# The guard for tiny weights of w_out and w3 on ScalarE, and the early stage's on-chip transfers begun from ScalarE's queue

## The chip, the cores and the metric

The kernel runs on one core of one Trainium2 chip. The metric is device microseconds of one execution. The engines are called PE (TensorE matmul; PEld is its weight load), DVE (VectorE), ACT (ScalarE), POOL (GpSimd) and SP (SyncE, which here only issues DMAs; its queue is SPq in the profile).

## What is computed

A block-causal attention over 8 batches, 8 heads, 576 positions and 64 columns a head (blocks of 64), and then a gated MLP on its output, all in float32:

```python
scores = scale * np.matmul(q, k.transpose(0, 1, 3, 2))
scores = np.where(mask, scores, -1000000000.0)      # mask: block_i >= block_j
attn = softmax(scores)                              # with 1e-09 added to the sum
x = np.matmul(attn, v)                              # as (4608, 512)
a = x @ w1                                          # w1, w2: (512, 1024)
b = x @ w2
h = a * b @ w3                                      # w3: (1024, 1024)
return h @ w_out                                    # w_out: (1024, 512)
```

q and k are drawn with a spread of about 0.4, v with 0.1. The weights arrive as float64, seen as pairs of 32-bit integers.

## The kernel before

The work goes by pairs of heads, n = 0 to 31, four to a batch; within a pair the heads are j = 0 and 1. A matmul with full precision is made of products of a high part (float32r) and a low part (the rest), as in the three products per weight tile in `gen_moe`.

**Two stages.** In the early stage, pairs 0 to 3 (`EARLY`), the attention of batch 0 runs beside the preparation of all weights (`gen_w`). `w_out` comes in 8 tiles, `w3` in 16 (two for each of eight columns of blocks, m = 0 to 7), `w1` and `w2` in 8 each: 40 tiles of 128 x 512 weights. For each m, eight products on PE (L358) make 128 rows of w3 x w_out, named w0 to w7; ACT and DVE split the sum into `wh` and `wl` (L346, L347). The first, w0, needs all of `w_out` and the two tiles of w3 for m = 0. In the late stage pairs 4 to 31 are mixed with the MLP of the batch before, and PE's order is the one in which the code is written. Its first MLP products (ab, L381) need xh and xl of pairs 0 to 3, the last of which is x of pair 3.

**One weight tile** (`load_w`, L122 to L143): SP issues the load into one of five `wraw` buffers; ACT takes the absolute value of the upper words (L135) into one of six `wbits` buffers; DVE raises it to at least 2^-15 (L136, the guard for tiny weights, which keeps the exponent of the next step from running below its range), shifts and masks it (L137), puts the sign and the top bit of the exponent in (L138) and adds three bits of the lower word (L141). For w1 and w2 the result goes on to ACT and DVE, which split it into high and low (L147, L148); for w_out and w3 it is used as it is.

**One pair of the early stage.** `shift_mask` finds the row maxima by products mx on PE and reductions m on DVE (L179, L183, L185), transposes them (mt, L187) and ACT writes them as `ms` (L189). `prep_qk` casts q and k to `qk` (L157), copies that high part to the other half of the partitions with a transfer inside the chip (qk<-qk, L206) and subtracts the low part on DVE (L207). `shift` writes `ms` as a row of `qk` with a second transfer inside the chip (qk<-ms, L196). Then PE forms s (L230), ACT exp (pe, L238), PE x (L269); DVE transposes the sums (tr, L309) and scales x (L320 to L323), and `finish_x` splits it into xh and xl (L332, L333). All these transfers, like the loads, stand in SP's queue.

**What sets the order.** In the early stage a scheduler orders each engine's instructions from the plans `EARLY_PLAN` and from priorities: steps of the attention go ahead of the weights. Each queue then runs in its order, and an instruction that waits holds up all behind it.

Of the kernel before, what the change touches and what calls it, by code (L numbers as in the profile page):

```python
# [7 lines left out]
F32 = mybir.dt.float32  # L8
# [3 lines left out]
AF = mybir.ActivationFunctionType  # L12
ALU = mybir.AluOpType
# [3 lines left out]
P = 128  # L17
B, H, S, D = 8, 8, 576, 64
BLK = 64
NB = S // BLK  # L20
# [8 lines left out]
EARLY = NPAIR  # L29
SCALE = 0.125  # L30
BIG = 8.0e9

# [24 lines left out]
def block_causal_attention__then__gated_mlp_kernel(ctx, tc, qkv, consts, ident_in, w1, w2, w3t, wout, out_t):  # L59
    nc = tc.nc  # L60
    w1, w2, w3t, wout = (w.bitcast(I32) for w in (w1, w2, w3t, wout))

    cpool = ctx.enter_context(tc.tile_pool(name="cpool", bufs=1))
# [18 lines left out]
    qk = [cpool.tile([P, 4, S], F32R, name=f"qk{j}") for j in range(2)]  # L82
# [28 lines left out]
    def open_late():  # L111
# [7 lines left out]
        tl["gh"] = pool.tile([P, NF, HALF], F32R, name="gh")  # L119
        tl["gl"] = pool.tile([P, NF, HALF], F32R, name="gl")  # L120

    def load_w(dst, src, k):  # L122

        t = tl["early"].tile([P, 1024], F32, tag="wraw", name="wraw", bufs=5)
        u = tl["early"].tile([P, 512], F32, tag="wbits", name="wbits", bufs=6)
        wide = t.bitcast(I32)
        nc.sync.dma_start(out=wide.rearrange("p (k w) -> p k w", k=k), in_=src)  # L130
        wide = wide.rearrange("p (c two) -> p c two", two=2)
        low, high = wide[:, :, 0], wide[:, :, 1]
        bits = u.bitcast(I32)
        V = nc.vector
        nc.scalar.activation(u, high.bitcast(F32), AF.Abs)  # L135
        V.tensor_scalar(out=u, in0=u, scalar1=2.0**-15, scalar2=None, op0=ALU.max)  # L136
        V.tensor_scalar(out=bits, in0=bits, scalar1=3, scalar2=0x3FFFFFF8, op0=ALU.logical_shift_left, op1=ALU.bitwise_and)  # L137
        V.scalar_tensor_tensor(out=bits, in0=high, scalar=-0x40000000, in1=bits, op0=ALU.bitwise_and, op1=ALU.bitwise_or)  # L138
        if dst is None:
            dst = u.unsqueeze(1)  # L140
        V.scalar_tensor_tensor(out=dst.bitcast(I32), in0=low.rearrange("p (k w) -> p k w", k=k), scalar=29,  # L141
                               in1=bits.rearrange("p (k w) -> p k w", k=k), op0=ALU.logical_shift_right, op1=ALU.bitwise_or)
        return u  # L143

    def load_split(dst_h, dst_l, src):
        val = load_w(None, src.unsqueeze(1), 1)
        nc.scalar.copy(dst_h, val)  # L147
        nc.vector.tensor_tensor(out=dst_l, in0=val, in1=dst_h, op=ALU.subtract)  # L148
# [6 lines left out]

    def cast(n, dst, src, act):
        (nc.scalar.copy if 0 < n <= EARLY or act else nc.vector.tensor_copy)(dst, src)  # L157

    ms_of = {}

    def shift_mask(n):
        r = raw_of[n]
        rqk = r[:, 0 : 2 * S].rearrange("p (t s) -> p t s", t=2)
        kb = work.tile([P, S], BF16, tag="kb", name=f"kb{n}")
        cast(n, kb, rqk[:, 1, :], CAST[1])
        for j in range(2):
            cast(n, qd[own[j], :, own[j]], rqk[own[j], 0, :].rearrange("p (i r) -> p i r", r=BLK), CAST[2])
# [21 lines left out]
        nc.scalar.mul(out=ms[0:NB], in_=mt[0:NB, 0:P], mul=-1.0)  # L189
        ms_of[n] = ms  # L190
        shift(n, 0)
        yield

    def shift(n, j):
        row = qk[j][oth[j].start : oth[j].start + 1, 1, :].rearrange("p (i r) -> p i r", r=BLK)
        nc.sync.dma_start(out=row.bitcast(F32), in_=ms_of[n][0:NB, j * BLK : (j + 1) * BLK].bitcast(F32))  # L196

    def prep_qk(n, j):
        rqk = raw_of[n][:, 0 : 2 * S].rearrange("p (t s) -> p t s", t=2)
        o, x = own[j], oth[j]  # L200
        if j == 1:
            shift(n, 1)
        high, low = qk[j][o, 0::3, :], qk[j][o, 1:3, :]
        cast(n, high, rqk[o], CAST[0])
        yield
        nc.sync.dma_start(out=qk[j][x, 0::2, :].bitcast(F32), in_=high.bitcast(F32))  # L206
        (nc.vector if n <= EARLY else nc.gpsimd).tensor_tensor(out=low, in0=rqk[o], in1=high, op=ALU.subtract)  # L207
        yield

# [126 lines left out]
    def gen_w(wp):  # L336
        wo = tl["wo"]
        for k in range(NF):
            load_w(wo[:, k : k + 1, :], wout[k * P : (k + 1) * P, :].unsqueeze(1), 1)
            yield  # L340
# [8 lines left out]
        for m in range(NF):  # L349
            t3 = wp.tile([P, NF, P], F32, tag="w3", name="w3", bufs=2)  # L350
            for k in range(0, NF, 4):
                src = w3t[k * P : (k + 4) * P, 2 * m * P : 2 * (m + 1) * P].rearrange("(k p) f -> p k f", p=P)
                load_w(t3[:, k : k + 4, :], src, 4)
                if k == 0:
                    yield
            acc = ps_m.tile([P, 512], F32, tag="psm", name=f"w{m}")
            for k in range(NF):
                nc.tensor.matmul(acc, t3[:, k, :], wo[:, k, :], start=(k == 0), stop=(k == NF - 1))  # L358
            pending.append((m, acc))
            if len(pending) > 1:  # L360
                evacuate()
            yield
            next(rows1)
            yield
# [48 lines left out]
    open_early(wp)  # L413
    fill(shift_mask(0), 100)
    fill(prep_qk(0, 0), 100)
    for j in range(2):
        prep_v(0, j)
# [3 lines left out]
    def pair(n):  # L421
# [5 lines left out]
        last = n + 1 == NN  # L427
        masks = iter(()) if last else shift_mask(n + 1)
        own_qk = prep_qk(n, 1)
        next_qk = iter(()) if last else prep_qk(n + 1, 0)  # L430
        for j in range(2):
            xps = ps_x.tile([P, 1024], F32, tag="psx", name=f"x{n}_{j}")
# [60 lines left out]
def _layout(q, k, v, moe_w1, moe_w2, moe_w3, moe_w_out):  # L493
# [12 lines left out]
    for c in range(4):  # L506
        consts[1 + c, 0, 2 * c * BLK : (2 * c + 1) * BLK] = 1.0
        consts[1 + c, 1, (2 * c + 1) * BLK : (2 * c + 2) * BLK] = -BIG
    return {
# [27 lines left out]
```

## Time and profile before

| | |
|---|---|
| median of 3 runs | 1007.41 us (1006.82 to 1007.84) |
| the profiled execution | 1008.37 us, its span 1006.6 us |
| PE busy | 961.6 us, 96% of the span |
| PEld busy | 886.1 us, 88% |
| DVE busy | 718.8 us, 71% |
| ACT busy | 547.9 us, 54% |
| POOL busy | 521.1 us, 52% |
| DMA | 80.39 MB, mean 80 GB/s |

The shares are means over both stages. The profile's slices of 25 us show DVE at 70 to 99% and DMA at 50 to 80% in the first five and DVE near 75% and DMA near 20% later. So a stage is read by itself: the busy time of each engine in a stretch, then the engine's rows in order of time, in which a bracket gives the idle time ahead of a row and what ended it. Busy times of neighbours overlap by a little, since the next instruction starts while the last one drains; what one of them adds in a full queue is the distance from start to start.

### The profile page before, as it was taken

The numbers are of one execution on the slowest core, as the hardware profiler recorded it, in microseconds if no ns is written. First come the engines' busy times: TensorE is split into PE (matmuls) and PEld (weight loads), VectorE is DVE, ScalarE is ACT, GpSimd is POOL, SyncE is SP. The second block draws the span as 40 slices with busy tenths as digits, with TensorE's granted clock in tenths as the row PEclk, the third lists the DMA queues.
The fourth block names the chain that finished last, engine by engine and source line by source line (L and its number), as shares of the span: only waits on it lengthen the run. The fifth ranks groups of instructions, "written<-read, shape, count | busy, mean of one in ns | idle before, by whom it ended". The sixth has DMA issues, their size and how long they took to land.

```text
span 1006.6 us, 18165 instructions
## 1 busy us (share of the span) xinstructions
PE 961.6 (96%) x6594; PEld 886.1 (88%) x6624; DVE 718.8 (71%) x1356; ACT 547.9 (54%) x1433; POOL 521.1 (52%) x525
## 2 busy tenths in 40 slices
PE   4699958999999999999999999999999999999998
PEld 2354548999999999999999999999999999999998
DVE  7999997767777777777777767777777777774100
ACT  4655755555565655555555566555555655653211
POOL 0000006667665766666666657576666766573211
PEclk9799978999999999999999999999999999999999
DMA  8776522122212221221222222212212222110000
GB/s 247 240 257 195 170 82 61 55 80 61 85 57 78 61 74 38 70 73 56 78 61 85 61 74 61 84 32 67 73 58 76 61 85 61 37 24 25 1 25 24
DMA packets 36409, 80.39 MB, mean 80 GB/s; under 512 B 4384, under 2 KB 20896, under 8 KB 36320
## 3 DMA queue, kind: packets, MB, share of 16 engines
q1 hardware_dynamic: 36320, 79.23, 26.5%
q8 instruction: 52, 0.85, 0.4%
q14 instruction: 37, 0.30, 0.1%
HBM read 50.76 MB, written 9.44 MB: 60 GB/s over the span
## 4 chain that ended last, share of the span: by engine, by line
PE 60%; DVE 23%; ACT 9%; issue 6%; DMA 2%; DVEq 0%; ACTq 0%
PE ab L381 23%; PE o L397 20%; DVE pl L248 7%; PE s L230 6%; PE x L285 4%; PE mx L179 3%; DVE g L388 2%; ACT ph L246 2%; PE w L358 2%; ACT p L245 2%; DVE m L183 2%; DVE wbits L138 1%; DVE x L323 1%; DVE rb L322 1%; DVE qk L157 1%
## 5 line engine op out<-in xcount | busy, mean ns | idle before, releaser
L251 POOL TENSOR_TENSOR rsum<-rsum,p 128x448 f32<-128x448 f32 x224 | 178.3, 796 | 120.4 <-ACT p L245 113.6
L248 DVE TENSOR_TENSOR pl<-p,ph 128x448 fp32r<-128x448 f32 x168 | 150.9, 911 | 64.1 <-ACT ph L246 63.2
L389 ACT CAST gh<-g 128x288 fp32r<-128x288 f32 x128 | 55.5, 433 | 219.3 <-DVE g L388 219.3
L390 POOL TENSOR_TENSOR gl<-g,gh 128x288 fp32r<-128x288 f32 x128 | 108.3, 846 | 123.0 <-ACT gh L389 122.9
L230 PE MATMUL s<-qk 128*128 128x288 f32 (+4 forms) x768 | 160.7, 317 | 9.2 <-DMA qk<-ms 3.5
L381 PE MATMUL ab<-xh,w1h 128*128 128x288 f32 x512 | 152.0, 297 | 6.8 <-ACT xh L332 6.8
L381 PE MATMUL ab<-xh,w2h 128*128 128x288 f32 x512 | 154.1, 301 | 0.0
L397 PE MATMUL o<-gh,wh 128*128 128x288 f32 x512 | 153.4, 300 | 0.0
L381 PE MATMUL ab<-xh,w1l 128*128 128x288 f32 x512 | 151.6, 296 | 0.0
L381 PE MATMUL ab<-xl,w2h 128*128 128x288 f32 x512 | 151.5, 296 | 0.0
L381 PE MATMUL ab<-xl,w1h 128*128 128x288 f32 x512 | 151.5, 296 | 0.0
L381 PE MATMUL ab<-xh,w2l 128*128 128x288 f32 x512 | 151.4, 296 | 0.0
L397 PE MATMUL o<-gl,wh 128*128 128x288 f32 x512 | 150.8, 295 | 0.0
L397 PE MATMUL o<-gh,wl 128*128 128x288 f32 x512 | 150.8, 295 | 0.0
L207 POOL TENSOR_TENSOR qk<-raw,qk 64x1152 fp32r<-64x1152 f32 x54 | 144.3, 2672 | 2.0
L220 POOL TENSOR_TENSOR vs<-raw,vs 128x320 fp32r<-128x320 f32 x56 | 49.9, 891 | 174.2 <-ACT vs L157 174.2
L230 PEld LDWEIGHTS s<-qk 128*128 128x128 f32 (+1 forms) x768 | 116.9, 184 | 26.1 <-issue 6.1
L183 DVE TENSOR_REDUCE m<-mx 128x1 f32<-128x512 f32 (+6 forms) x320 | 128.6, 449 | 15.8 <-PE mx L179 13.2
L246 ACT ACTIVATE ph<-s 128x288 fp32r<-128x288 f32 x336 | 131.3, 392 | 0.0
L388 DVE TENSOR_TENSOR g<-ab,a 128x288 f32<-128x288 f32 x128 | 57.7, 451 | 74.4 <-PE ab L381 71.2
L245 ACT ACTIVATE p<-s 128x448 f32<-128x448 f32 x224 | 85.5, 382 | 45.8 <-PE s L230 44.2
L285 PE MATMUL x<-ph,vs 128*128 128x128 f32 x336 | 104.1, 319 | 0.0
(71 smaller groups left out, 2141.6 us busy)
## 6 DMA issues: line engine op xcount, KB each, us to landing
raw<-in_qkv SPq DMA_DIRECT2D x32, 896.0 KB
qk<-qk SPq DMA_DIRECT2D x64, 288.0 KB
out_t<-o SPq DMA_DIRECT2D x64, 144.0 KB
wraw<-in_w3t SPq DMA_DIRECT2D x16, 512.0 KB
wraw<-in_w SPq DMA_DIRECT2D x16, 512.0 KB
wraw<-in_wout SPq DMA_DIRECT2D x8, 512.0 KB
qk<-ms SPq DMA_DIRECT2D x64, 2.2 KB
cst<-in_consts SPq DMA_DIRECT2D x1, 288.0 KB
```

The source lines that it names most:

```text
L183: nc.vector.reduce_max(m[:, col : col + 1], sc, axis=AX.X)
L207: (nc.vector if n <= EARLY else nc.gpsimd).tensor_tensor(out=low, in0=rqk[o], in1=high, op=ALU.subtract)
L230: nc.tensor.matmul(t[ks, at : at + q1 - q0], qk[j][:, 2 + s, kr], qk[j][:, s, q0:q1], start=(s == 0), stop=(s == 1))
L245: nc.scalar.activation(p32, t[ks, at : at + w], AF.Exp, scale=SCALE)
L246: nc.scalar.activation(ph[ks, o : o + w], t[ks, at : at + w], AF.Exp, scale=SCALE)
L248: nc.vector.tensor_tensor(out=low, in0=p32, in1=ph[ks, o : o + w], op=ALU.subtract)
L251: nc.gpsimd.tensor_tensor(out=r, in0=r, in1=p32, op=ALU.add)
L285: nc.tensor.matmul(xps[:, to : to + w], v[:, c, :], pr[:, a : a + w], start=(u < 2 and s == 0), stop=(u in (0, len(PV) - 1) and s == len(p ...
L381: nc.tensor.matmul(t[:, 0:HALF], l[:, c, fs], r, start=(c == 0 and s == 0), stop=(c == NC - 1 and s == 2))
L388: nc.vector.tensor_tensor(out=g32, in0=acc[1][:, 0:HALF], in1=a32, op=ALU.mult)
L390: nc.gpsimd.tensor_tensor(out=gl[:, f, :], in0=g32, in1=gh[:, f, :], op=ALU.subtract)
L397: nc.tensor.matmul(t[:, 0:HALF], l[:, f, es], r[:, f, :], start=(f == 0 and s == 0), stop=(f == NF - 1 and s == 2))
```

## The change

For w_out and w3 (where `load_w` is given a destination) the guard becomes one ACT instruction on the upper 16 bits of each word, seen as unsigned integers: relu(top - 0x3800), with the constant in a new tile `floor` of one column. The subtracted bits are among those that the next step masks out. For w1 and w2 the guard stays on DVE. The transfers inside the chip, L206 and L196 before, are issued from ACT's queue for pairs 0 to 4 and from SP's for the rest.

```diff
+U16 = mybir.dt.uint16
...
+    floor = cpool.tile([P, 1], F32, name="floor")
+    nc.vector.memset(floor, -float(0x3800))
...
         nc.scalar.activation(u, high.bitcast(F32), AF.Abs)
-        V.tensor_scalar(out=u, in0=u, scalar1=2.0**-15, scalar2=None, op0=ALU.max)
+        if dst is None:
+            V.tensor_scalar(out=u, in0=u, scalar1=2.0**-15, scalar2=None, op0=ALU.max)
+        else:
+            top = u.bitcast(U16).rearrange("p (c two) -> p c two", two=2)[:, :, 1]
+            nc.scalar.activation(top, top, AF.Relu, bias=floor)
...
+    def queue(n):
+
+        return nc.scalar if n <= EARLY else nc.sync
...
-        nc.sync.dma_start(out=row.bitcast(F32), in_=ms_of[n][0:NB, j * BLK : (j + 1) * BLK].bitcast(F32))
+        queue(n).dma_start(out=row.bitcast(F32), in_=ms_of[n][0:NB, j * BLK : (j + 1) * BLK].bitcast(F32))
...
-        nc.sync.dma_start(out=qk[j][x, 0::2, :].bitcast(F32), in_=high.bitcast(F32))
+        queue(n).dma_start(out=qk[j][x, 0::2, :].bitcast(F32), in_=high.bitcast(F32))
```

The scheduler makes a new order of it on every engine. In the names below, s0_1 is s of pair 0, head 1, and the last number is that of a buffer; lines are those of the kernel in question. First ACT around the mask row ms of pair 1, before:

```order
L238 ACTIVATE pe0_1_280<-s0_1_309 128x320
L238 ACTIVATE pe0_1_280<-s0_1_322 128x192
L238 ACTIVATE pe0_1_280<-s0_1_322 64x64
L157 CAST qk1_85<-raw1_147 64x2x576
L135 ACTIVATE wbits_294<-wraw_293 128x512
L216 COPY ve1_144<-raw1_147 128x5x64
L135 ACTIVATE wbits_315<-wraw_314 128x512
L135 ACTIVATE wbits_330<-wraw_329 128x512
L189 ACTIVATE ms1_272<-mt1_270 9x128
L135 ACTIVATE wbits_392<-wraw_391 128x512
L157 CAST kb2_375<-raw2_353 128x576
L157 CAST qd_88<-raw2_353 64x9x64 x2
```

and after the change:

```order
L251 ACTIVATE pe0_1_282<-s0_1_311 128x320
L140 ACTIVATE wbits_332<-wraw_331 128x512
L202 ACTIVATE ms1_274<-mt1_272 9x128
L145 ACTIVATE wbits_332<-wbits_332,floor_97 128x512
L209 DMA qk0_84<-ms1_274 1x9x64
L251 ACTIVATE pe0_1_282<-s0_1_324 128x192
L251 ACTIVATE pe0_1_282<-s0_1_324 64x64
L166 CAST kb2_377<-raw2_355 128x576
L166 CAST qd_88<-raw2_355 64x9x64
L140 ACTIVATE wbits_394<-wraw_393 128x512
L166 CAST qd_88<-raw2_355 64x9x64
```

The transfer qk0<-ms1 is now ACT's, right behind the guard of the second w3 tile (wbits_332); the cast of qk1 and the copy ve1 have gone behind these rows, and kb and qd of pair 2 stand behind that guard.

PE around the first product of w3 and w_out, w0, before:

```order
L230 MATMUL s1_0_379<-qk0_84 128x288
L269 MATMUL x0_1_279<-pe0_1_280,ve1_144 128x192
L230 MATMUL s1_0_383<-qk0_84 128x288
L269 MATMUL x0_1_279<-pe0_1_280,ve1_144 128x64
L187 MATMUL mt1_270<-ident_79,m1_213 9x128
L358 MATMUL w0_337<-wo_100,w3_313 128x512 x8
L230 MATMUL s1_0_383<-qk0_84 128x288
L230 MATMUL s1_0_379<-qk0_84 128x288
L358 MATMUL w1_422<-wo_100,w3_405 128x512
```

and after:

```order
L282 MATMUL x0_1_281<-pe0_1_282,ve1_146 128x448
L243 MATMUL s1_0_381<-qk0_84 128x288
L282 MATMUL x0_1_281<-pe0_1_282,ve1_146 128x320
L371 MATMUL w0_339<-wo_102,w3_315 128x512 x8
L282 MATMUL x0_1_281<-pe0_1_282,ve1_146 128x192
L243 MATMUL s1_0_385<-qk0_84 128x288
L282 MATMUL x0_1_281<-pe0_1_282,ve1_146 128x64
L243 MATMUL s1_0_381<-qk0_84 128x288
L243 MATMUL s1_0_385<-qk0_84 128x288
L371 MATMUL w1_424<-wo_102,w3_407 128x512 x2
```

Two products of x of pair 0 and one of s of pair 1 have gone behind w0, and its mt ahead of them (not in the rows any more).

DVE around the first two tiles of w3 (w3_313 before, w3_315 after), before:

```order
L141 SCALAR_TENSOR_TENSOR wo_100<-wraw_293,wbits_294 128x512
L138 SCALAR_TENSOR_TENSOR wbits_315<-wraw_314,wbits_315 128x512
L136 TENSOR_SCALAR wbits_330<-wbits_330 128x512
L141 SCALAR_TENSOR_TENSOR w3_313<-wraw_314,wbits_315 128x512
L137 TENSOR_SCALAR wbits_330<-wbits_330 128x512
L309 STREAM_TRANSPOSE tr0_1_355<-x0_1_279 64x576
L138 SCALAR_TENSOR_TENSOR wbits_330<-wraw_329,wbits_330 128x512
L310 TENSOR_SCALAR rr0_150<-tr0_1_355 64x18
L136 TENSOR_SCALAR wbits_392<-wbits_392 128x512
L141 SCALAR_TENSOR_TENSOR w3_313<-wraw_329,wbits_330 128x512
```

and after:

```order
L147 SCALAR_TENSOR_TENSOR wbits_317<-wraw_316,wbits_317 128x512
L146 TENSOR_SCALAR wbits_332<-wbits_332 128x512
L150 SCALAR_TENSOR_TENSOR w3_315<-wraw_316,wbits_317 128x512
L147 SCALAR_TENSOR_TENSOR wbits_332<-wraw_331,wbits_332 128x512
L150 SCALAR_TENSOR_TENSOR w3_315<-wraw_331,wbits_332 128x512
L142 TENSOR_SCALAR wbits_394<-wbits_394 128x512
```

Between the guard's neighbours there is no L136 any more, and the transpose tr of pair 0, head 1, which stood between the two tiles of w3, has gone behind the next tiles. As counted over the whole order, 16 guards are left on DVE (L142 after the change), 24 are on ACT (L145), and ACT has 20 transfers (10 of L209 and 10 of L219).

## Rows read from the trace of the kernel before

**Rows 1.** Stretches: length; busy PE, PEld, DVE, ACT, POOL; clock; DMA share; GB/s
```profile
11.50:41.60 30.10, 17.91 (x69) 11.03 (x67) 28.93 (x64) 17.79 (x35) 0.00 (x0) 0.92 0.81 253
40.00:45.00 5.00, 3.24 (x4) 1.52 (x5) 4.88 (x12) 3.30 (x6) 0.00 (x0) 0.50 0.87 286
41.60:153.00 111.40, 97.40 (x313) 52.76 (x316) 108.18 (x219) 65.15 (x127) 2.15 (x2) 0.91 0.57 176
41.70:138.00 96.30, 93.58 (x300) 49.69 (x303) 93.82 (x192) 59.14 (x116) 0.00 (x0) 0.96 0.64 200
153.50:1006.60 853.10, 844.53 (x6209) 821.55 (x6236) 576.03 (x1069) 459.76 (x1264) 516.75 (x516) 1.00 0.20 59
```
**Rows 2.** Timeline of PE: start, length, instruction, count, idle before and its end
```profile
34.36 0.49 PE L269 MATMUL x<-pe,ve 128*128 128x192 f32 x2
...
34.91 0.43 PE L269 MATMUL x<-pe,ve 64*128 64x64 f32 x2
...
41.76 9.58 PE L358 MATMUL w<-wo,w 128*128 128x512 f32 x16 [4.41 <-DVE w L141]
...
61.65 7.11 PE L358 MATMUL w<-wo,w 128*128 128x512 f32 x16
...
85.19 0.96 PE L230 MATMUL s<-qk 128*128 128x448 f32 x4 [0.48 <-ACT pe L238]
...
102.78 0.59 PE L269 MATMUL x<-pe,ve 128*128 128x192 f32 x2 [0.54 <-ACT pe L238]
...
114.71 0.40 PE L230 MATMUL s<-qk 128*128 128x288 f32 x1 [0.24 <-ACT pe L238]
...
129.86 0.79 PE L230 MATMUL s<-qk 128*128 128x288 f32 x4 [0.70 <-DVE qk L207]
...
143.43 1.09 PE L230 MATMUL s<-qk 128*128 128x288 f32 x3 [3.50 <-DMA qk<-ms]
...
153.50 0.61 PE L381 MATMUL ab<-xh,w1h 128*128 128x288 f32 x1 [6.82 <-ACT xh L332]
```
**Rows 3.** Timeline of DVE
```profile
33.64 1.36 DVE L207 TENSOR_TENSOR qk<-raw,qk 64x1152 fp32r<-64x1152 f32 x1 [0.66 <-ACT qk L157]
...
114.38 0.76 DVE L136 TENSOR_SCALAR wbits<-wbits 128x512 f32<-128x512 f32 x2
...
130.56 0.78 DVE L309 STREAM_TRANSPOSE tr<-x 64x576 f32<-64x576 f32 x1
...
151.24 1.42 DVE L323 TENSOR_TENSOR x<-x,rb 128x576 f32<-128x576 f32 x1
```
**Rows 4.** Groups by line to 153.5 us: count, busy us, mean ns, idle before
```profile
L136 DVE TENSOR_SCALAR wbits<-wbits 128x512 f32<-128x512 f32 x40 | 16.5, 417 | 0.3 <-ACT wbits L135 0.3
...
L135 ACT ACTIVATE wbits<-wraw 128x512 f32<-128x512 f32 x40 | 26.9, 677 | 19.0 <-DMA wraw<-in_w3t 9.4 <-DMA wraw<-in_w 4.9 <-DMA wraw<-in_wout 2.5
```
**Rows 5.** Stretches for one line alone, L136 on DVE, L135 on ACT
```profile
11.50:41.60 30.10, 4.18 (x10) 0.92 0.81 253
...
11.50:41.60 30.10, 6.45 (x10) 0.92 0.81 253
```
**Rows 6.** Issues on SP to 160 us: count, shortest, median, longest ns
```profile
L196 SPq DMA_DIRECT2D qk<-ms x10: 751/794/887, 17.1 to 141.7; - x10
...
L206 SPq DMA_DIRECT2D qk<-qk x10: 602/660/687, 6.5 to 137.2; - x10
```
**Rows 7.** Timeline of ACT
```profile
32.46 1.15 ACT L157 CAST qk<-raw 64x1152 fp32r<-64x1152 f32 x1
...
35.38 0.46 ACT L216 COPY ve<-raw 128x320 f32<-128x320 f32 x1 [1.07 <-PE x L269]
...
37.56 0.65 ACT L135 ACTIVATE wbits<-wraw 128x512 f32<-128x512 f32 x1
...
39.85 0.67 ACT L157 CAST kb<-raw 128x576 bf16<-128x576 f32 x1 [1.63 <-DMA raw<-in_qkv]
40.42 1.35 ACT L157 CAST qd<-raw 64x576 bf16<-64x576 f32 x2
```

## The prediction

> **What bounds the kernel now.** I read the table by stretch first. After 153.5 us PE is busy for 844.5 of 853.1 us, so that part is bound by TensorE; its order is fixed, and the change moves only its start [rows 1]. What can move is the first 153.5 us. There the same table shows two different regimes. From 11.5 to 41.6 us DVE is busy for 28.9 of 30.1 us and PE for 17.9: the weights are being unpacked and PE waits for the first block of w3 with all of w_out. From 41.7 to 138 us both are full, PE 93.6 and DVE 93.8 of 96.3 us. Then DVE alone is full again until x of pair 3 is scaled, while PE idles.
>
> The timeline of PE says the same in rows. It waits 4.41 us for DVE's first w3 tile and begins the products w = w_out x w3 at 41.76; from there to 129.86 its idle pieces are 0.48, 0.54, 0.24 and 0.70 us, 2.0 us in 88 [rows 2]. So in that stretch nothing that makes DVE faster can give more than 2.0 us: PE has no more idle time to lose. After it PE waits 3.5 us and then 6.82 us for xh, which hangs on DVE's product x at 151.24 [rows 2, 3]. This is the second place where DVE decides.
>
> **Part 1: the guard goes from DVE to ACT, 24 of 40 times.** L136 costs 417 ns on average, but two in a row take 0.76 us, so a further one adds 0.34 us: that is its price in a full queue [rows 3, 4]. 24 of them are 8.2 us of DVE. Ten lie ahead of the first w3 tile, 8 for w_out and 2 for w3, 10 x 0.34 = 3.4 us; they are the ten of the stretch to 41.6 [rows 5]. The other 14, 4.8 us, lie beside a full PE and can give at most the 2.0 us above.
>
> On ACT no row has a 16-bit integer operand. The nearest is the Abs on the same 512 columns, L135, 677 ns [rows 4]; below it stands its share in a full queue, 10 in 6.45 us [rows 5]; above it I allow twice 677 ns, since nothing shows that a 16-bit, every-second-element operand is as fast. I take 677, as operation, columns and partitions are those of the row. That makes 24 x 0.68 = 16.3 us more of ACT. The guard also stands between Abs and DVE's shift, one more ACT instruction of latency for each tile; six buffers of wbits cover it as long as ACT runs ahead.
>
> The Trainium skill, "ScalarE: Activation LUTs", Rules for kernel authors, tells one to do relu and max on VectorE, not on ScalarE. The durations above agree with it, and by it alone the move would cost 24 x (0.677 - 0.417) = 6.2 us of engine time and end at 1013.6 us.
>
> **Part 2: 20 transfers begin on ACT.** On SP one issue of qk<-qk takes 660 ns and one of qk<-ms 794 ns [rows 6]. The after kernel has ten of each on ACT, 14.5 us; no row shows an issue on ACT, so the bounds are nothing (it passes while the instruction ahead still runs) and those durations plus the cast's own length where the issue waits for the cast just ahead; I take SP's durations. SP is freed of the same 14.5 us and of its waits for casts and masks, so weights and the next pair's raw tile are asked for earlier. DVE waited 0.3 us for an Abs in all of this part [rows 4], so I cost that at nothing; what hides it is the wraw ring, five tiles ahead of DVE.
>
> **The sum up to w.** ACT worked 17.8 us of the stretch to 41.6 [rows 1]. Ten guards (6.8) and six issues (4.4) come to it, and by the new order the cast of qk1, the copy ve, one Abs and the casts kb and qd of pair 2, 4.1 us within this stretch, stand behind the guard of the second w3 tile instead of in it [rows 7]. That is 24.9 us. DVE's stretch could shrink by 3.4 us and, as the low part of qk1 (1.36 us and a wait of 0.66) has also moved behind that tile, by 5.4 us [rows 3]. The other bound is nothing, if ACT's waits stay as they were (12.3 us in this stretch). I take 2.8, about the middle: it leaves ACT 27.3 us for 24.9 us of work and 2.4 us of waiting. Against it stands PE's new order: two products of pair 0's x and one of s1_0 have come behind w0; the like of them took 0.49 and 0.43 us before [rows 2], and I take 0.7 us for the three. In the same place DVE's transpose tr of (0,1) now waits until w0 is over, with the next w3 tile queued behind it; I take this as covered by w1's first four products and s1_0's.
>
> **From w to the end.** PE is full and may win back 0 to 2.0 us; I take 1.0. ACT had 65.1 us of work in the 111.4 us from 41.6 to 153 [rows 1]; 14 guards (9.5) and 14 issues (10.2) make 84.8. In a queue in order some of that comes ahead of an exp that PE waits for: between nothing and 14 x 0.73 = 10.2 us; I take 1.0, near the low end, because PE has w products between the exps. In the tail, from tr at 130.56 to x at 151.24 [rows 3], DVE carries 20.7 us; the new order has two steps of a w2 tile (0.6 us each) ahead of that place, where DVE then waits for PE anyway. I take 1.0 of 1.2.
>
> Sum: 2.8 - 0.7 + 1.0 - 1.0 + 1.0 = 3.1 us. The profiled execution took 1008.4 us, of which its span is 1006.6; 3.1 off gives 1005.3. The median of the runs is 1007.4, 1.0 below the profiled one, so the forecast is **1004.3 us**.
>
> **Rivals.** *DVE's whole saving comes through.* For it: DVE is the one that PE waits for at 41.76. If w begins 5.4 us earlier, and PE's clock, 0.50 in the 5 us from 40 [rows 1], is full for w0 so that its 16 records take 7.1 us as at 61.65 instead of 9.6 [rows 2], the sum is 5.4 - 0.7 + 1.0 + 2.5 = 8.2: 999.2 us. Against it: ACT would have 24.7 us for 24.9 us of work.
>
> *Nothing measurable.* ACT sets the pace until w0, so that the 2.8 is lost, and the rest cancels: 1.0 - 1.0 + 1.0 - 0.7 = 0.3, so 1007.1 us. For it: the 24.9 us above leave little for waits. Against it: 2.4 us of idle ACT are left even with the gain.
>
> *Slower: PE waits for exps behind ACT's issues.* The place is 42 to 130 us, the wait that of PE's s for pe and of x for pe, and the price 0.73 us for each of the 14 issues that stands ahead of such an exp. It turns the sign from the sixth on (6 x 0.73 = 4.4 against 3.1 + 1.0); with ten it is 7.3 - 4.1 = 3.2 slower, 1010.6 us. For it: the waits for pe were 0.24 to 0.54 us a piece, so PE has little cover where s follows s [rows 2]. Against it: ACT is idle for 46 of the 111 us. By the Trainium skill's rule above ("ScalarE: Activation LUTs", Rules for kernel authors) the time would come out on this side too.
>
> That the change does not do what it says I give no chance of its own: the order has 16 guards left on DVE, 24 on ACT, and no issue of the first four pairs on SP. A guard twice as dear as taken (16 us more of ACT) goes with the slower rival.
>
> **How the numbers follow.** Forecast, a gain of 2.0 to 5.5 us: 0.46. The whole saving: 0.12. Nothing: 0.21. Slower: 0.21. A measurement here can tell about 0.2%, 2.0 us, from no change, so faster is 0.46 + 0.12 = 0.58, same 0.21, slower 0.21. The range of 8 in 10 goes from 999.0, with the whole saving in it, to 1010.8, past the slower rival at ten issues; what is left out is the dearer half of that rival and a gain beyond DVE's 8.2.
>
> **What would show it.** In the profile after: w begins near 39 us instead of 41.76 and is followed by PE idle of under 3 us up to the last s of pair 3; L141 of the first w3 tile ends near 38; DVE falls below 93% in the stretch that was full, since PE holds it; x of pair 3 near 148; ACT busy some 105 us before it. A guard on ACT of 0.6 to 0.7 us and an issue of 0.6 to 0.8 us would show the prices right. The forecast is wrong if PE's waits for pe sum to more than 4 us, if w still begins at 41 us or later, or if DVE's idle time before Abs and guard exceeds 3 us in the first 42 us.

## The result, and the profile after

The changed kernel takes **1009.99 us** (median of 15 runs, 1005.53 to 1014.34) beside 1007.59 (15 runs, 1004.62 to 1010.18) for the kernel before: a ratio of **1.0028 [1.0016, 1.0040]**. It is slower by 0.28%. The forecast was 1004.3 and faster. The profiled execution took 1009.57 us, its span 1007.8, which is 1.2 more than before's span. So the pair of profiles shows half of the 2.4 us between the medians. The changed kernel also spreads over 8.8 us where before spreads over 5.6, so no single profile of it stands for the whole difference.

The stretches after, in the columns of [rows 1], with two that tell where the time went:

```profile
11.50:41.60 30.10, 19.42 (x68) 11.78 (x68) 26.27 (x56) 21.98 (x42) 0.00 (x0) 0.89 0.75 247
40.00:45.00 5.00, 4.89 (x13) 2.08 (x12) 3.92 (x7) 3.42 (x6) 0.00 (x0) 1.00 0.88 261
62.00:84.00 22.00, 20.57 (x75) 11.00 (x73) 20.76 (x43) 16.21 (x32) 0.00 (x0) 1.00 0.67 205
98.00:114.00 16.00, 13.29 (x43) 6.75 (x42) 12.91 (x29) 9.73 (x18) 0.00 (x0) 0.89 0.49 146
153.50:1006.60 853.10, 845.61 (x6236) 824.33 (x6236) 575.24 (x1069) 459.55 (x1261) 516.09 (x516) 1.00 0.20 59
```

The same two middle stretches before:

```profile
62.00:84.00 22.00, 21.97 (x77) 11.86 (x76) 21.84 (x48) 13.89 (x28) 0.00 (x0) 1.00 0.60 181
98.00:114.00 16.00, 15.46 (x57) 8.24 (x57) 15.90 (x35) 10.05 (x20) 0.00 (x0) 1.00 0.49 153
```

Ahead of w0 DVE is down from 28.9 to 26.3 us of 30.1: the guards have left it. In the middle PE has lost what it had: 1.4 us of work less in 62 to 84, and 2.2 less in 98 to 114, there also at a granted clock of 0.89 where it had 1.00. DVE is no longer full in 98 to 114 either, 12.9 us where it had 15.9: it waits, too.

PE's timeline after, with the rows that answer to [rows 2]:

```profile
40.53 7.13 PE L371 MATMUL w<-wo,w 128*128 128x512 f32 x16
...
48.78 1.88 PE L371 MATMUL w<-wo,w 128*128 128x512 f32 x4
...
71.15 1.06 PE L243 MATMUL s<-qk 128*128 128x448 f32 x4 [0.86 <-ACT pe L251]
...
103.27 0.59 PE L282 MATMUL x<-pe,ve 128*128 128x192 f32 x2 [2.71 <-ACT pe L251]
...
104.83 6.00 PE L371 MATMUL w<-wo,w 128*128 128x512 f32 x10
...
122.63 3.59 PE L371 MATMUL w<-wo,w 128*128 128x512 f32 x8
...
143.52 0.66 PE L243 MATMUL s<-qk 128*128 128x288 f32 x3 [2.22 <-DMA qk<-ms]
...
153.82 0.61 PE L394 MATMUL ab<-xh,w1h 128*128 128x288 f32 x1 [8.44 <-ACT xh L345]
```

The rows before of the second and the last group of w:

```profile
51.76 1.12 PE L358 MATMUL w<-wo,w 128*128 128x512 f32 x2
...
120.39 4.45 PE L358 MATMUL w<-wo,w 128*128 128x512 f32 x10
```

w0 begins at 40.53 where it began at 41.76 [rows 2], and w1 at 48.78 where it began at 51.76: 3.0 us are won. The last group of w7 begins at 122.63 where it began at 120.39: from w1 on 5.2 us are lost. The tail gives 1.9 of that back, so that ab begins 0.3 us later than before. The other 0.9 us of the span lie behind 153.8 us, where the change touches only pair 4; no run here tells whether they belong to it.

The largest wait between w0 and the last of w7, 2.71 us at 103.27, is for exps on ACT. This is ACT's timeline just ahead of it:

```profile
98.69 0.67 ACT L140 ACTIVATE wbits<-wraw 128x512 f32<-128x512 f32 x1 [0.79 <-DMA wraw<-in_w3t]
99.40 0.87 ACT L145 ACTIVATE wbits<-wbits,floor 128x512 uint16<-128x512 uint16 x1
100.14 0.55 ACT L359 CAST wh<-w 128x512 fp32r<-128x512 f32 x1
...
101.81 0.67 ACT L140 ACTIVATE wbits<-wraw 128x512 f32<-128x512 f32 x1 [1.12 <-DMA wraw<-in_w]
102.38 0.61 ACT L156 CAST w1h<-wbits 128x512 fp32r<-128x512 f32 x1
102.89 0.43 ACT L251 ACTIVATE pe<-s 128x192 f32<-128x192 f32 x2
```

The exps (pe) stand last. Two Abs ahead of them wait for loads that are still under way, 0.79 and 1.12 us, and guard, wh and w1h stand between. No transfer is issued here at all: the new order put an instruction that waits for memory in front of one that PE needs.

The groups by line to 155 us (count, busy us, mean ns, idle before and what ended most of it):

```profile
L145 ACT ACTIVATE wbits<-wbits,floor 128x512 uint16<-128x512 uint16 x24 | 20.1, 865 | 0.2
...
L146 DVE TENSOR_SCALAR wbits<-wbits 128x512 int32<-128x512 int32 x40 | 16.5, 422 | 3.0 <-ACT wbits L145 2.9
...
L196 DVE TENSOR_REDUCE m<-mx 128x1 f32<-128x512 f32 (+7 forms) x50 | 20.2, 450 | 5.6 <-PE mx L192 5.3
```

The guard takes 865 ns on ACT. DVE waits 2.9 us for it and 5.3 us for the products mx of PE, where it waited 0.3 and 0.2 before. Up to the start of x of pair 3, 152.49 us where it was 151.24, DVE's busy time went from 141.3 to 134.8 us and its idle time from 9.9 to 17.7. **The change took 6.5 us of work from DVE, and 7.8 us of waiting came in its place.**

### The profile page after: what moved, and what is told of

It reads as the page before. It is cut to its first block, busy times and chain, and to the rows that moved or that the text cites. A ratio compares the mean times of both kernels' runs of the same rounds, so it can differ in the third digit from the quotient of the medians.

```text
span 1007.8 us, 18183 instructions
## 1 busy us (share of the span) xinstructions
PE 961.0 (95%) x6624; PEld 887.7 (88%) x6624; DVE 711.0 (71%) x1333; ACT 565.3 (56%) x1457; POOL 520.3 (52%) x525
## 4 chain that ended last, share of the span: by engine, by line
PE 56%; DVE 24%; ACT 10%; issue 6%; DMA 4%; DVEq 0%; ACTq 0%
PE ab L394 21%; PE o L410 20%; DVE pl L261 7%; PE s L243 6%; PE x L298 4%; PE mx L192 3%; DVE g L401 3%; ACT ph L259 2%; DMA wraw<-in_w3t 2%; ACT p L258 2%; DVE m L196 2%; DVE x L336 2%; DVE rb L335 1%; DVE qk L166 1%; ACT xh L345 1%
## 5 line engine op out<-in xcount | busy, mean ns | idle before, releaser
L196 DVE TENSOR_REDUCE m<-mx 128x1 f32<-128x512 f32 (+6 forms) x320 | 128.4, 449 | 21.9 <-PE mx L192 19.9
L394 PEld LDWEIGHTS ab<-xh,w1h 128*128 128x128 f32 x512 | 96.5, 189 | 9.1 <-ACT xh L345 8.7
```

The source lines that it names most:

```text
L196: nc.vector.reduce_max(m[:, col : col + 1], sc, axis=AX.X)
L394: nc.tensor.matmul(t[:, 0:HALF], l[:, c, fs], r, start=(c == 0 and s == 0), stop=(c == NC - 1 and s == 2))
```

## The experiments

A first theory was that the new order of the instructions makes the loss (O in the expectations); its rivals were that the transfers inside the chip get slower because a freed SP sends more loads beside them (C), and that the issues themselves hold ACT up (A; other letters are explained where they stand). All ratios are to the kernel before on the same chip. Diffs are against the changed kernel unless they say otherwise.

### The two halves

**Guard on ACT, transfers back on SP.**

```diff
-        queue(n).dma_start(...)
+        nc.sync.dma_start(...)      # in shift and in prep_qk
```

> Only the guard's move; all transfers stay on SP. In DVE's order the last step of the w1 tile stands here ahead of the low part wl of w5 again, as in the kernel before. Theory O (order: the loss is the place at 98 to 104 us where wl of w5 stands ahead of that step, so that the exps behind the cast of w1h come 2.7 us late, and the clock falls after it): no such stall, w begins 1 to 3 us earlier than in the kernel before, time 1004.0 to 1006.5. Rival L (load: ACT has 20.6 us of guards in front of masks and exps, whatever the order): the guard alone already costs, 1008.5 to 1011. Rival Q (the transfers on ACT are what costs): 1005 to 1007, and the queue alone is slower than before.

1005.87 us, 0.9985 [0.9974, 0.9996]: faster than before, and the lowest ratio of all kernels run, though the intervals of four others overlap with its own.

**Transfers on ACT, guard back on DVE.**

```diff
-        if dst is None:
-            V.tensor_scalar(out=u, in0=u, scalar1=2.0**-15, ...)
-        else:
-            ...
-            nc.scalar.activation(top, top, AF.Relu, bias=floor)
+        V.tensor_scalar(out=u, in0=u, scalar1=2.0**-15, ...)
```

> Only the transfers' move; the guard stays on DVE everywhere. Theory O: the issues mostly run beside ACT's other instructions, 0 to 3 us, so 1007 to 1010, and whichever place has wl ahead of a w1 step shows the wait. Rival L: no guard on ACT, so like the kernel before, 1006.5 to 1008.5. Rival Q: 20 issues of 0.65 to 0.77 us, some in front of exps: 1009.5 to 1013.

1013.41 us, 1.0061 [1.0046, 1.0076]. So the guard is the half that gains, 0.15%, and the transfers are the half that loses, each in the order that the scheduler makes of it.

**The kernel before without the guard of w_out and w3** (that step is left out).

```diff
-        V.tensor_scalar(out=u, in0=u, scalar1=2.0**-15, ...)
+        if dst is None:
+            V.tensor_scalar(out=u, in0=u, scalar1=2.0**-15, ...)
```

> The kernel before with the guard of w_out and w3 left out: neither DVE nor ACT does it (24 instructions of DVE gone, nothing put on ACT), transfers on SP. It gives the most that taking the guard from DVE can bring. Theory O: w begins 3 to 5 us earlier and PE gains up to 2.5 us more by a full clock in w0: 999 to 1003. If the gain is under 2 us, the step that was wrong is the worth of DVE's saving itself and not its price on ACT.

1006.64 us, 0.9993 [0.9982, 1.0004]. Even when nobody does these 24 instructions, the time falls by 0.7 us, and the interval holds no change. w0 begins at 39.33, 2.4 us earlier, and DVE gives it back in 5.6 us of waits for PE's mx. So little is the saving on DVE worth, in the order that comes with it. The guard on ACT measured 0.8 us less than no guard, but the intervals overlap and the two orders differ, so how much of its 1.5 us is the order's doing is not shown.

**The guard on POOL** (in the kernel before).

```diff
-        V.tensor_scalar(out=u, ...)
+        (V if dst is None else nc.gpsimd).tensor_scalar(out=u, ...)
```

> The guard of w_out and w3 on POOL, which is idle in the early stage, as a maximum on 32-bit words; transfers on SP. It takes the 24 instructions from DVE without putting them on ACT. If ACT's load by the guards is what the guard alone still pays for: 1004 to 1005.5. If the saved DVE time has no taker, as when the guard was left out altogether (1006.6): 1006 to 1007. If POOL's price for 512 columns (no row here) is over 1.5 us, DVE waits for it: 1007 or more.

1013.9 us, 1.0066 [1.0044, 1.0088]. The groups by line to 155 us show what this move cost; the order is a new one here too:

```profile
L136 POOL TENSOR_SCALAR wbits<-wbits 128x512 f32<-128x512 f32 x24 | 40.4, 1690 | 61.7 <-ACT wbits L135 56.0 <-DVE m L183 5.7
...
L137 DVE TENSOR_SCALAR wbits<-wbits 128x512 int32<-128x512 int32 x40 | 18.9, 479 | 5.2 <-POOL wbits L136 5.1
```

One guard takes 1690 ns on POOL where DVE took 417 [rows 4], DVE waits 5.1 us for it, and DVE's own next step on the same tile, L137, takes 479 ns on average where it took 418. An idle engine is not a free one.

### Is it ACT's time, or one place?

**The transfers on POOL's queue**, so that ACT issues none of them.

```diff
-        return nc.scalar if n <= EARLY else nc.sync
+        return nc.gpsimd if n <= EARLY else nc.sync
```

> The changed kernel with the 20 transfers begun by POOL, idle there, and not by ACT. The guard alone gave 1005.9 and the transfers alone cost 6 us, so the question is what of moving them costs. Theory C (collision: SP, freed of the transfers, issues weight loads earlier, three at 2.3 us where it was one, and these share the DMA engines with pair 0's tile, its copies and its mask, so that the first s comes at 13.9 us and not 10.7): SP is freed in the same way, time 1008.5 to 1011. Theory A (ACT's queue: 0.65 to 0.77 us an issue, and what stands behind it): ACT has none, time 1005 to 1007.

1013.17 us, 1.0056 [1.0040, 1.0072]: worse with ACT's queue clear of them. So a loss doesn't need issues on ACT. But the order differs here as well (PE waits 4.91 us for exps at 52.51), so this does not show that ACT's issues cost nothing.

**The two steps that follow a w group exchanged**, `evacuate()` (wh, wl) behind the next w1 tile, to take the 2.71 us wait away.

```diff
-            if len(pending) > 1:
-                evacuate()
             yield
             next(rows1)
+            if len(pending) > 1:
+                evacuate()
```

> The changed kernel with the split of the block before (wh, wl) written after the w1 tile instead of ahead of it. In DVE's order the last step of the w1 tile then stands ahead of wl of w5. Theory O: the wait of PE for the exp of pair 2 (2.71 us at 103 us) is gone and the clock stays full behind it; 3 to 4 us less than the changed kernel, 1005.5 to 1007. Rivals L and Q: the load on ACT is the same, so the time stays within 1 us of the changed kernel, 1009 to 1011, and the wait shows up at another exp.

1013.96 us, 1.0062 [1.0044, 1.0080]. The wait of 2.71 us fell to 1.01, at 105.45, but one of 2.29 us for pe came at 73.26. This expectation failed: a new order took one wait and made another, and the kernel is slower than the changed one (1.0028) by 0.34%.

**The same exchange in the kernel before.**

> The kernel before with the split of the block before (wh, wl) written after the w1 tile: no instruction more or less, none on another engine, only another order from the scheduler. It measures what an order alone moves. Theory S: 2 us or more in either direction from 1007.4. Theories A and C: within 1 us of it.

1006.39 us, 0.9989 [0.9979, 0.9998]. Here nothing but the order differs. The same exchange took 1.1 us off this kernel and put 3.4 us on the changed one: an order alone moves the time by amounts like those in question, either way.

**Pair 0's transfers on SP.**

```diff
-        return nc.scalar if n <= EARLY else nc.sync
+        return nc.scalar if 0 < n <= EARLY else nc.sync
```

> The changed kernel with pair 0's four transfers back on SP and those of pairs 1 to 4 on ACT. Theory C: the second weight load stands behind the copy again, the first s is back near 11 us; most of the cost is gone, 1005.5 to 1007.5. Theory A: 16 of 20 issues are still on ACT, 1009 to 1010.5.

1011.04 us, 1.0037 [1.0019, 1.0055]: no gain, although the first s is back at 10.83. The order is a new one again (the last of w7 begins at 125.28), so what pair 0's transfers cost by themselves is not read from it.

**The second and third weight load held back** until the first copy has landed, by a one-element write of POOL into their buffers that reads `qk`.

```diff
+        held.append(t)
+        if len(held) in (2, 3):
+            nc.gpsimd.tensor_copy(t[D : D + 1, 0:1], qk[0][D : D + 1, 0, 0:1].bitcast(F32))
         nc.sync.dma_start(out=wide.rearrange("p (k w) -> p k w", k=k), in_=src)
```

> The changed kernel with the second and third weight load held until the first copy of qk has landed, by a one-element write of POOL to their buffers that reads what the copy wrote; everything else as changed, ACT's issues too. Theory C: the first s comes near 11 us instead of 13.9; 2 to 3 us less than the changed kernel, 1007 to 1008. Theory A: nothing gained, 1009.5 to 1011.

1010.57 us, 1.0031 [1.0016, 1.0045]. PE's first s stayed at 13.68, since products mx stand ahead of it in PE's order. So the kernel doesn't test what it was made for, whether an earlier first s brings the time back; the kernel above had one, and gained nothing.

**Only the copies qk<-qk on SP**, in the order that the scheduler makes of it.

```diff
-        queue(n).dma_start(out=qk[j][x, 0::2, :].bitcast(F32), ...)
+        nc.sync.dma_start(out=qk[j][x, 0::2, :].bitcast(F32), ...)
```

> The changed kernel with the ten copies qk<-qk back on SP and only the ten mask rows qk<-ms on ACT. Theory C: the copies hold back SP's loads as before, 1005.5 to 1007.5. Theory A: half of the issues are left on ACT, about half of the cost, 1007.5 to 1008.5; if the masks are the ones that stand in front of exps and casts, 1009 or more.

1009.17 us, 1.0014 [1.0001, 1.0026]. Half of the loss is gone, but the order differs as well.

### Order and queue apart

Every edit so far changed the order too. The next kernels hold it still: a table gives for PE, DVE, ACT and SP's loads the instruction numbers in the order of another kernel, and this loop at the end makes the scheduler keep it, by an edge of order without a semaphore (lines then stand 8 lower):

```diff
+    by = {i.name: i for i in nc.cur_bb.bb.instructions}
+    for row in ORDER:
+        for a, b in zip(row, row[1:]):
+            tc.add_manual_dep(by[f"I-{b}"], f"I-{a}", mybir.DependencyInfo(mybir.DependencyClass.NoSync, ...), reason="order")
```

**The changed kernel in the order of the one with the guard alone:**

> The changed kernel, transfers begun by ACT, but with PE, DVE, ACT and SP's loads held in the order which the scheduler made for the guard alone (1005.9); the 20 issues are put in where they become ready. Theory S (order: moving the transfers lets the scheduler make another order, and that costs the 4 us): 1004.5 to 1007. Theory A (ACT's issues themselves) or C (loads that SP asks for earlier): the issues and the freed SP are as in the changed kernel, 1009 to 1011.

**The guard alone in the changed kernel's order:**

> The other way about: transfers begun by SP as in the guard alone, but PE, DVE, ACT and SP's loads held in the order of the changed kernel. Theory S: as slow as the changed kernel, 1009 to 1012. Theories A and C: no issue on ACT and SP's loads behind its transfers again, 1005 to 1007.

**The transfers alone in the order of before:**

> Only the transfers on ACT, guard on DVE (1013.4 in its own order), held in the order of the kernel before on PE, DVE, ACT and SP's loads. Theory S: back at the kernel before, 1006.5 to 1008.5. Theory A: 20 issues on ACT in front of exps and casts, 1010 to 1013.5. Theory C: the same, from the loads that come earlier.

| transfers begun from | guard-alone order | changed kernel's order |
|---|---|---|
| SP | 0.9985 [0.9974, 0.9996] | 1.0026 [1.0015, 1.0038], 1010.09 us |
| ACT | 1.0019 [1.0010, 1.0027], 1008.98 us | 1.0028 [1.0016, 1.0040] |

The third kernel, the guard on DVE and all in the order of before, gives 1.0032 [1.0020, 1.0045], 1010.11 us. So the transfers on ACT cost 3.4 us (0.34% of 1007) in the one order, 3.2 in before's and 0.2 in the changed kernel's; and the new order costs 4.1 us with the transfers on SP, 0.9 with them on ACT. **Either alone makes nearly the whole difference of 4.3 us; together they make hardly more.** Both first theories were half right. No run holds a kernel in its own order unaltered, so what the holding itself costs is not measured; the nearest, the guard-alone kernel held with only two exps moved (below), is 0.8 us above the unheld one.

### Which transfers

In the order of the guard alone, first **the masks qk<-ms on SP, the copies on ACT**, then **the copies on SP, the masks on ACT**:

```diff
-        queue(n).dma_start(out=row.bitcast(F32), ...)
+        nc.sync.dma_start(out=row.bitcast(F32), ...)
```

> Transfers of masks (qk<-ms) back on SP, copies (qk<-qk) on ACT, everything held in the order of the guard alone, in which all transfers on SP gave 1005.9 and all on ACT 1009.0. Theory M (masks: begun by ACT, they come behind weight loads that SP has sent ahead, 5.4 us from issue to the s that waits instead of 2.4, and the first issue holds ACT 1.3 us): the 3 us are gone, 1005 to 1007. Theory K (copies, or the freed SP queue as such): still 1008 to 1010.

```diff
-        queue(n).dma_start(out=qk[j][x, 0::2, :].bitcast(F32), ...)
+        nc.sync.dma_start(out=qk[j][x, 0::2, :].bitcast(F32), ...)
```

> The other half: copies back on SP, masks on ACT, in the same order. Theory M: the 3 us stay, 1008 to 1010, and s of pair 1 waits more than 3 us for its mask before the first block w0. Theory K: 1005 to 1007.

1007.43 us, 0.9999 [0.9989, 1.0009], and 1010.87 us, 1.0032 [1.0022, 1.0042]. With 0.9985 for none moved and 1.0019 for both, the masks cost 4.7 us beside copies on SP and 2.0 beside copies on ACT; the copies cost 1.4 at most. It is the masks.

The traces show two ways in which they lose. First the write of pair 1's mask, SP's issues and PE's next s with the guard alone:

```profile
34.29 0.27 ACT L202 ACTIVATE ms<-mt 9x128 fp32r<-9x128 f32 x1
...
34.59 0.81 SPq L209 DMA_DIRECT2D qk<-ms  x1
...
35.49 0.67 SPq L135 DMA_DIRECT2D wraw<-in_w  x1
...
36.22 0.41 SPq L95 DMA_DIRECT2D raw<-in_qkv  x1
...
37.00 0.53 PE L243 MATMUL s<-qk 128*128 128x288 f32 x2 [1.64 <-DMA qk<-ms]
...
40.59 1.38 PE L243 MATMUL s<-qk 128*128 128x448 f32 x3 [3.06 <-ACT pe L251]
41.77 8.86 PE L371 MATMUL w<-wo,w 128*128 128x512 f32 x16
```

Then the same order with the transfers on ACT, from pair 0's mask on:

```profile
17.47 1.33 ACTq L217 DMA_DIRECT2D qk<-ms  x1
...
18.85 0.66 ACT L148 ACTIVATE wbits<-wraw 128x512 f32<-128x512 f32 x1 [0.71 <-ACT qd L174]
...
34.37 0.34 SPq L143 DMA_DIRECT2D wraw<-in_w  x1
...
34.76 0.42 SPq L103 DMA_DIRECT2D raw<-in_qkv  x1
...
36.21 0.27 ACT L210 ACTIVATE ms<-mt 9x128 fp32r<-9x128 f32 x1
...
36.51 0.74 ACTq L217 DMA_DIRECT2D qk<-ms  x1
...
41.96 0.85 PE L251 MATMUL s<-qk 128*128 128x288 f32 x2 [4.69 <-DMA qk<-ms]
...
43.07 1.38 PE L251 MATMUL s<-qk 128*128 128x448 f32 x3 [0.26 <-ACT pe L259]
44.25 8.99 PE L379 MATMUL w<-wo,w 128*128 128x512 f32 x16
```

*The mask lands late.* On SP the mask goes out at 34.59 and the two loads have to queue behind it; s follows 2.4 us after its issue. With the mask on ACT, SP sends both loads at 34.37 and 34.76, and s follows the mask's issue at 36.51 only after 5.45 us, behind them. At 141.64 in the changed kernel, with no load left, s follows its mask's issue after 1.9 us. So the transfer itself is no slower from ACT; it is slow behind loads.

*The first issue is long.* Not all of w0's 2.5 us (44.25 where it was 41.77) is this one mask: the mask row was written 1.9 us later already, at 36.21 instead of 34.29. In pair 0 the first issue on ACT takes 1.33 us from 17.47, and the next Abs begins only when it is over, at 18.85, after 0.71 us of idle ACT. DVE then waits 0.99 us for the guard behind that Abs, where it waited 0.20, and pair 0's s behind its mask begins at 21.98 where it began at 20.90. The rest is 0.3 us of later start and 0.8 by which the row of six x products behind it is longer (3.48 us where it was 2.65). And of the 3.0 us by which the wait for pair 1's mask is longer, 2.8 would have been waited anyway: with the guard alone PE waits 3.06 us for exps that stand behind Abs and guards on ACT, and here only 0.26. So in this pair of kernels the late mask of pair 1 is mostly hidden, and what w0 lost came mainly in pair 0.

In other orders PE stands ready for pair 0's mask and waits for it, 1.30 us in the changed kernel and 1.34 with only the masks on ACT. These are rows from the chains that ended last (start, length, what): of the changed kernel, of the transfers alone in the order of before, and two of the kernel with only the masks on ACT, whose w0 begins at 46.36:

```profile
17.69 4.63 DMA qk<-ms
```

```profile
17.23 3.87 DMA qk<-ms
```

```profile
17.50 6.07 DMA qk<-ms
...
38.53 5.50 DMA qk<-ms
```

With the masks on SP no profile of these kernels has PE waiting for pair 0's mask. No run issues a mask from SP behind the same loads, so that the loads and not ACT's queue make it late is read from the mask of 1.9 us, not tested apart.

By the Trainium skill, "DMA: Bandwidth & Descriptors", in the section "Issuing engines are not separate DMA queues", transfers begun from any engine run on the same 16 DMA engines, and several issuing engines save only the issuing time. The traces agree: a mask without loads takes 1.9 us from either queue (138.09 to 139.95 from SP with the guard alone), and those from ACT behind loads, where PE waited for them, 3.9 to 6.1.

### The order's price at one place

**The changed kernel in its own order, with only the place of the 2.71 us wait altered**: on ACT, wh of w5 ahead of the next w3 tile, and w1h and the two exps ahead of the Abs that waits for its load; on DVE, the last step of the w1 tile ahead of m and of wl of w5.

> The changed kernel held in its own order but for one place: on DVE the last step of the w1 tile stands ahead of the maximum and of wl of w5, on ACT wh of w5 ahead of the next w3 tile, and w1h with the two exps of pair 2 ahead of the next absolute value. Theory P (that place is what its order loses): the wait of 2.71 us at 103 us shrinks under 1, 2 to 3 us off, 1007 to 1008. Theory R (one place is not it; the time comes back at the next wait): within 1 us of the changed kernel, 1009 to 1011.

1007.82 us, 1.0007 [0.9999, 1.0016]: 2.1 us better than the changed kernel, and no longer to be told from before. PE's and ACT's timelines at that place:

```profile
101.33 0.59 PE L290 MATMUL x<-pe,ve 128*128 128x192 f32 x2
...
102.64 0.32 PE L200 MATMUL mx<-kb,qd 128*128 128x384 bf16 x1 [0.71 <-DVE m L204]
```

```profile
100.47 0.59 ACT L164 CAST w1h<-wbits 128x512 fp32r<-128x512 f32 x1
100.96 0.43 ACT L259 ACTIVATE pe<-s 128x192 f32<-128x192 f32 x2
...
101.84 0.66 ACT L148 ACTIVATE wbits<-wraw 128x512 f32<-128x512 f32 x1 [0.45 <-DMA wraw<-in_w]
```

x comes at 101.33 with no wait, 1.9 us earlier than in the changed kernel; the Abs still waits for its load, but behind the exps, and the granted clock from 98 to 114 is 1.00 again (it is 0.89 in the guard-alone kernel too). This is the one place whose price was taken out by itself, and it is most of what the changed kernel lost against before.

**The changed kernel's order up to w0 and the guard-alone order from the second block on.**

> The changed kernel, transfers on ACT, held in its own order up to the first block w0 and from the second block on in the order of the guard alone. If its order loses in the middle (w0 to the last block took 82 us there, 78 in the order of the guard alone) and gains only ahead of w0: 1005 to 1007. If what is lost in the middle belongs to the issues on ACT: 1009 to 1011.

1012.37 us, 1.0043 [1.0030, 1.0056]. It missed: PE waits 3.89 us for DVE's tile at 57.38 and 1.14 at 43.72, where the two orders meet, so the kernel says nothing of either half.

**The same exchange of exps and Abs in the guard-alone kernel**, which has a wait of 1.54 us at 101.73.

> A version meant to beat both: the guard alone on ACT (transfers on SP, 1005.9), held in its own order but with the two exps of pair 2 at 101 us ahead of the two absolute values which wait for their loads there. Theory P (such places of ACT's order are lost one by one and add up): PE's wait of 1.54 us at 101.7 goes, 1 to 1.5 us off, 1004.3 to 1005. Theory R (what is won there is waited for at the next place): 1005.5 to 1006.5.

1007.09 us, 0.9993 [0.9985, 1.0002]: no gain over 0.9985. PE's timeline shows the next wait in its place:

```profile
103.47 0.32 PE L200 MATMUL mx<-kb,qd 128*128 128x384 bf16 x1 [1.55 <-DVE m L204]
```

With the guard alone the wait for ACT covered one of the same length for DVE; in the changed kernel the one behind it was only 0.71.

## Why the prediction was wrong

**The step that failed** is the −1.0 us for ACT's lateness, taken at the low end of 0 to 10.2 "because PE has w products between the exps". It priced issues in front of exps. No issue stood there; the new order put an Abs that waits for a load in front of them, once, for 2.71 us, and with the clock of the products behind it that place made 2.1 of the changed kernel's time. With that place altered the kernel is at 1.0007: the place turns the sign, and that no gain is left either is the matter of the 2.8 us below. PE's waits for pe from 42 us to the one at 130.33 sum to 0.86 + 2.71 + 0.61 = 4.2 us, past the 4 us named as the sign of a wrong forecast. The order shown ahead of the prediction had only the places near w0; this one stood 60 us later.

**The second failure** is in Part 2: "SP is freed of the same 14.5 us and of its waits for casts and masks, so weights and the next pair's raw tile are asked for earlier … so I cost that at nothing; what hides it is the wraw ring". The loads did go earlier, the raw tile of pair 2 at 12.33 us where it was 32.45. But SP's queue had been doing something that the forecast did not see: its order kept loads behind the masks. Freed, they are in front of them, and a mask that PE waits for takes 3.9 to 6.1 us where it took 1.9 to 3.4. The wraw ring hides nothing of it, since PE's s waits for the mask, not for a weight. Together with the long first issue on ACT this costs 3.4 us in the order of the guard alone and 3.2 in that of before. In the changed kernel's own order it costs 0.2, within the noise, so by itself it does not explain this kernel's loss: from the guard alone at 1005.9 us either failure leads up to about where the changed kernel is.

The steps one by one:

- **w0 2.8 us earlier, less 0.7 for the products behind it.** 1.2 measured at w0. At w1 it is 3.0, more than the 2.1 of the sum, but by the clock: w0's 16 records took 7.13 us where they took 9.58 [rows 2], at a clock of 1.00 (0.50 in [rows 1]). PE had been busy for 6.65 of the 7 us from 34 to 41, at 0.61, where before it was busy for 1.62 of them, at 0.92. I had put that gain only in the rival of the whole saving. The 2.8 itself fails with the guard alone: w0 begins at 41.77 there, as before, since PE's 4.41 us for DVE became 3.06 for exps behind Abs and guards. That is the bound of nothing, "if ACT's waits stay as they were".
- **+1.0 from PE's idle time between, −1.0 for ACT.** Net 0 expected, −5.2 measured from w1 to the last of w7. This is the mis-sized pair. Of it the place at 103 us is 2.1 of the time; the masks are hardly part of it, as 5.8 us are lost in the same stretch with the transfers on SP in this order (50.24 to 124.71). The rest was not taken apart.
- **+1.0 in the tail.** +1.9 measured between the last of w7 and ab. x of pair 3 still came at 152.49, not near 148, since the loss ahead of it was larger.
- **The guard at 677 ns** (645 to 1354): 865, so 24 are 20.1 us of ACT's busy time instead of 16.3. Within the bounds, and not decisive: with it alone the kernel gains 1.5 us. The Trainium skill's rule that I set beside it ("ScalarE: Activation LUTs", Rules for kernel authors) has the engine time right, 24 x (0.865 − 0.417) = 10.8 us more. By it alone the time would be longer, and that sign the runs don't bear out.
- **The issues at 660 and 794 ns**: 660 and 765 on ACT (medians), as taken, but for the first mask's 1320.
- **DVE's idle time for Abs and guard under 3 us in the first 42**: 1.7, as named.

The rival *slower: PE waits for exps behind ACT's issues* gave 1010.6 us, close to the 1010.0 measured, and the wait was the one that it named, PE's for pe. Its mechanism was another: at the longest of these waits no issue stood ahead of the exps. The number was met for the wrong reason, by luck. DVE's saving had about the value that *nothing measurable* gave it: 0.7 us with the guard left out altogether, an interval with no change in it.

**What stays open.** Why the order's 4.1 and the transfers' 3.4 us don't add up was not taken apart. Against the guard alone the changed kernel wins 1.2 us up to w0 and loses 3.8 from there to the last group of w7 (82.1 us there, 78.6 before, 78.3 with the guard alone). In its order no s waits for pair 1's mask, and with the transfers on SP w0 comes later, at 41.99, not earlier; that may be why the queue costs nothing there. Nor was it found which part of the guard's 865 ns is the 16-bit operand and which the tile `floor`, nor where the half of the difference lies that the profiled pair doesn't show.

## What to carry to other kernels

A queue's order is also a throttle: before small transfers are moved to another queue, read which loads it kept behind them, since those will be in front. After a scheduler has made a new order, go through it for the whole stage and look on each engine for an instruction that waits for memory ahead of one that the bound engine needs. What a change saves on an engine is known only with what that engine will wait for next; leaving the work out altogether, in one run, gives a first measure of it, in the order that comes with it.

## What the runs showed of the hardware

- A mask row of 576 elements takes 1.9 us from issue to use with no load under way, and, issued from ACT behind loads, 3.9 to 6.1 us; where the loads had to queue behind the mask it took 2.4 (guard alone) and 3.4 (masks on SP, copies on ACT: 35.32 to 38.67).
- The first mask issued on ACT took 1320 ns, 1.7 times the median of the ten (765), and held the cast behind it up for 0.83 us:

```profile
17.69 1.32 ACTq L209 DMA_DIRECT2D qk<-ms  x1
...
19.05 1.35 ACT L166 CAST qd<-raw 64x576 bf16<-64x576 f32 x2 [0.83 <-issue]
```

- On ACT the guard on 16-bit halves took 865 ns beside 671 for the Abs on the same 512 columns; on POOL a guard took 1690 ns beside 417 on DVE, and while POOL did it, DVE's L137 rose from 418 to 479 ns.
